# Loading x as bf16 by casting GpSimd DMAs straight into the transpose layout

## The chip, the cores and the metric

The kernel runs on one core of one Trainium2 chip. The time is device microseconds of one execution, as the median of several. The profile's "span", from the first to the last instruction that it records, is about 1.7 us shorter. On names: PE is TensorE, PEld its weight loads, DVE VectorE, ACT ScalarE, POOL GpSimd, SP SyncE.

## The reference

```python
# x: [8, 4096, 192] f32; weight: [8 heads, 7]; w_in: [192, 2048]; w_out: [2048, 192]
w   = softmax(weight, axis=-1)                      # per head, 7 taps
a   = causal_conv(x, w)                             # the 24 channels of a head share 7 taps
h   = a.reshape(32768, 192) @ w_in
out = maximum(0.01 * h, h) @ w_out                  # [32768, 192] f32
```

## The kernel before

The work goes in 32 blocks. A block is 512 positions of two batch rows (`e` = 0, 1). It goes through these steps: load x as f32 (`x_nat`), cast it to bf16 (`x_bf`), transpose it on PE (`ptr`), copy it out of PSUM on DVE (`xt`), convolve on DVE (`yt`), then mm1 on PE (`ph`), leaky ReLU on ACT (`g`), mm2 on PE (`po`), copy on DVE (`o_sb`) and store. x is prepared two blocks ahead of mm1.

```python
def load_x(blk):                       # SP queue, two DMAs of 384 KB, rows of 768 B
    t = stage_pool.tile([128, 2, SUB, D], FP32, name="x_nat")
    for e in range(2):
        nc.sync.dma_start(out=t[:, e, :, :],
            in_=x[2 * rp + e, st * ST : (st + 1) * ST, :].rearrange("(c p) d -> p c d", p=128))
def cast_x(blk, e, copy, half=None):   # x_bf is [128, SUB=4, NCH=3, 2, CH=64]
    copy(out=x_bf[blk][:, s, :, e, :], in_=x_nat[blk][:, e, s, :].rearrange(...))
def transpose_x(blk):                  # 24 transposes; x_bf is the stationary operand
    for s in range(SUB):
        for c in range(NCH):
            for i in range(2):
                ps = slice(i * CH, (i + 1) * CH)
                nc.tensor.transpose(out=ts[i][:, s, c, :],
                    in_=x_bf[blk][ps, s, c, :, :].rearrange("p e k -> p (e k)"),
                    identity=ident[ps, ps])
# ... start: x of blocks 0 and 1, then w_in in four quarters on the SP and ACT queues
load_x(2)                                                   # SP queue, behind w_in
# ... w_in cast on ACT; w_out loaded by a casting GpSimd DMA; 40 warm-up matmuls on PE
for blk in range(NBLK + 1):
    for j in range(STEPS):             # 8 steps
        # ... mm1 and g of blk (two f per step), mm2 of blk - 1
        if blk + 2 < NBLK:
            if j == 0: load_x(blk + 3)
            if 2 <= j < 6: cast_x(blk + 2, j % 2, nc.scalar.copy, half=(j - 2) // 2)
            if j == 7:
                transpose_x(blk + 2)
                evac_x(blk + 2, nc.vector.tensor_copy)
        # ... three of the 21 convolution steps of blk + 1 on DVE
```

Each transpose reads `e` and `k` as one row of 128 elements. This is why `x_bf` keeps them side by side, and why the load must hit this layout if it is to skip the cast.

Of the kernel before, what the change touches and what calls it, by code (L numbers as in the profile page):

```python
# [10 lines left out]
BF16 = mybir.dt.bfloat16  # L11
# [3 lines left out]
def kernel(  # L15
# [8 lines left out]
    nc = tc.nc  # L24
# [10 lines left out]
    CH = 64  # L35
    NCH = D // CH
    ST = 512
    SUB = ST // 128
    NFC = F // 128
    NB = S // ST  # L40
    NBLK = (B // 2) * NB
# [4 lines left out]
    WQ = 4  # L46

    const_pool = ctx.enter_context(tc.tile_pool(name="const", bufs=1))
    stage_pool = ctx.enter_context(tc.tile_pool(name="stage", bufs=3))
    xb_pool = ctx.enter_context(tc.tile_pool(name="xb", bufs=2))  # L50
    xt_pool = ctx.enter_context(tc.tile_pool(name="xt", bufs=2))
    yt_pool = ctx.enter_context(tc.tile_pool(name="yt", bufs=3))
    g_pool = ctx.enter_context(tc.tile_pool(name="g", bufs=3))
# [9 lines left out]
    x_nat, x_bf, xt, ptr = {}, {}, {}, {}  # L63

    def load_x(blk):
        if blk >= NBLK:
            return
        rp, st = divmod(blk, NB)
        t = stage_pool.tile([128, 2, SUB, D], FP32, name="x_nat")
        for e in range(2):  # L70
            nc.sync.dma_start(  # L71
                out=t[:, e, :, :],
                in_=x[2 * rp + e, st * ST : (st + 1) * ST, :].rearrange(
                    "(c p) d -> p c d", p=128
                ),
            )
        x_nat[blk] = t

    def cast_x(blk, e, copy, half=None):
        if blk not in x_bf:  # L80
            x_bf[blk] = xb_pool.tile([128, SUB, NCH, 2, CH], BF16, name="x_bf")
        s = slice(0, SUB) if half is None else slice(half * SUB // 2, (half + 1) * SUB // 2)
        copy(  # L83
            out=x_bf[blk][:, s, :, e, :],
            in_=x_nat[blk][:, e, s, :].rearrange("p s (c k) -> p s c k", c=NCH),
        )

    def transpose_x(blk):


        ts = [psum_o.tile([128, SUB, NCH, CH], BF16, name=f"ptr{i}", tag="po") for i in range(2)]
# [4 lines that stand above are left out]
                    nc.tensor.transpose(  # L96
                        out=ts[i][:, s, c, :],
                        in_=x_bf[blk][ps, s, c, :, :].rearrange("p e k -> p (e k)"),
                        identity=ident[ps, ps],
                    )  # L100
        ptr[blk] = ts

    def evac_x(blk, copy):
        rp, st = divmod(blk, NB)
        if st == 0:
            xt[rp] = xt_pool.tile([128, NCH, HALO + S], BF16, name="xt")
            nc.vector.memset(xt[rp][:, :, 0:HALO], 0.0)
        dst = xt[rp][:, :, HALO + st * ST : HALO + (st + 1) * ST].rearrange(
            "p c (s i k) -> p i s c k", s=SUB, i=2
        )  # L110
        for i, t in enumerate(ptr.pop(blk)):
            copy(out=dst[:, i], in_=t)  # L112


    yt = {}

    def conv_jobs(blk):
        rp, st = divmod(blk, NB)
        y = yt_pool.tile([128, NCH, ST], BF16, name="yt")
        yt[blk] = y  # L120
        jobs = []
        for c in range(NCH):
            for k in range(K):
                src = xt[rp][:, c, BASE + k + st * ST : BASE + k + (st + 1) * ST]
                dst = y[:, c, :]
                if k == 0:
                    jobs.append(
                        lambda s=src, d=dst, c=c: nc.vector.tensor_scalar_mul(  # L128
                            d, s, wk[:, c, 0:1]
                        )  # L130
                    )
                else:
                    jobs.append(
                        lambda s=src, d=dst, c=c, k=k: nc.vector.scalar_tensor_tensor(  # L134
                            out=d, in0=s, scalar=wk[:, c, k : k + 1], in1=d,
                            op0=mybir.AluOpType.mult, op1=mybir.AluOpType.add,
                        )
                    )
        return jobs
# [12 lines left out]
    for sign, off in ((1, 0), (-1, GRP - 1)):  # L152
        nc.gpsimd.affine_select(
            out=sel, in_=sel, compare_op=mybir.AluOpType.is_ge, fill=0.0,
# [11 lines left out]
        out=nmax, in_=w8, axis=mybir.AxisListType.X,  # L166
# [3 lines left out]
        out=w8, in_=w8, func=mybir.ActivationFunctionType.Exp, bias=nmax, scale=1.0,  # L170
    )
    nc.vector.tensor_reduce(
        out=ssum, in_=w8, axis=mybir.AxisListType.X, op=mybir.AluOpType.add,
# [5 lines left out]
    for c in range(NCH):  # L179
        nc.tensor.matmul(  # L180
            out=wps[:, 0, c * K : (c + 1) * K],
# [5 lines left out]
        out=wk, in_=wps[:, 0, 0 : NCH * K].rearrange("p (c k) -> p c k", c=NCH)  # L187
# [4 lines left out]
    cast_x(0, 1, nc.scalar.copy)  # L192
    transpose_x(0)
    evac_x(0, nc.vector.tensor_copy)
    for job in conv_jobs(0):
        job()

    w_stage = g_pool.tile([128, NCH, F], FP32, name="w_stage", tag="g")
    for q in range(WQ):
        for e in range(2):  # L200
            fs = slice(q * F // WQ, (q + 1) * F // WQ)
            (nc.sync, nc.scalar)[e].dma_start(
                out=w_stage[e * CH : (e + 1) * CH, :, fs],
                in_=moe_w_in[:, fs].rearrange("(c p) f -> p c f", p=CH),
            )
    load_x(2)

    cast_x(1, 0, nc.scalar.copy)
    cast_x(1, 1, nc.scalar.copy)
    transpose_x(1)  # L210
    evac_x(1, nc.scalar.copy)

    w_in = const_pool.tile([128, NCH, F], BF16)
# [6 lines left out]
    nc.gpsimd.tensor_copy(out=pjunk, in_=w_stage[0:1, NCH - 1, F - 1 : F])  # L220
    w_out = const_pool.tile([128, NFC, D], BF16)
    nc.gpsimd.dma_start(out=w_out, in_=moe_w_out.rearrange("(c p) d -> p c d", p=128))  # L222


    wa = psum_h.tile([128, 2, ST], FP32, name="warm", tag="ph")
    NWARM = 40
    for i in range(NWARM):
        nc.tensor.matmul(  # L228
            out=wa[:, 0, :], lhsT=ident, rhs=xt[0][:, 0, HALO : HALO + ST],
# [6 lines left out]
    def mm1(blk, f):  # L236
        y = yt[blk]
        ph = psum_h.tile([128, 2, ST], FP32, name="ph", tag="ph")
        for c in range(NCH):
            for e in range(2):  # L240
                ps = slice(e * CH, (e + 1) * CH)
                nc.tensor.matmul(  # L242
                    out=ph[:, e, :],
                    lhsT=w_in[ps, c, f * 128 : (f + 1) * 128],
                    rhs=y[ps, c, :],
                    start=(c == 0),
                    stop=(c == NCH - 1),
                )
        return nc.scalar.activation(  # L249
            out=g[blk][:, f, :, :], in_=ph,  # L250
            func=mybir.ActivationFunctionType.Prelu, alpha=0.01,
        )
# [25 lines left out]
    def mm2(n):  # L278


        if n <= LAST:
            for fc in range(NFC if n < LAST else LAG):
                if n < LAST:
                    mm2_one(0, n, fc)
                t1 = n * NFC + fc - LAG
                if t1 >= 0:
                    mm2_one(1, *divmod(t1, NFC))
                    if t1 % NFC == NFC - 1:
                        evac_o(t1 // NFC)
        if n >= LAST:  # L290
            for fc in range(NFC):
                mm2_one(None, n, fc)
            evac_o(n)
# [16 lines left out]
    for blk in range(NBLK + 1):  # L310
        if blk < NBLK:
            g[blk] = g_pool.tile([128, NFC, 2, ST], BF16, name="g", tag="g")
        jobs = conv_jobs(blk + 1) if blk + 1 < NBLK else []
        for j in range(STEPS):
            n = (blk - 1) * STEPS + j
            if blk < NBLK:
                for f in range(FPS * j, FPS * (j + 1)):
                    act = mm1(blk, f)
                    if f == FPS * j:
                        seal[n] = act.ins.name  # L320
            if n >= 0:
                mm2(n)
            if blk + 2 < NBLK:
                if j == 0:
                    load_x(blk + 3)
                if 2 <= j < 6:
                    cast_x(blk + 2, j % 2, nc.scalar.copy, half=(j - 2) // 2)
                if j == 7:
                    transpose_x(blk + 2)
                    evac_x(blk + 2, nc.vector.tensor_copy)  # L330
            for job in jobs[3 * j : 3 * (j + 1)]:
                job()

# [29 lines left out]
```

## Time and profile before

| | before |
|---|---|
| time, median of 3 | 718.55 us (718.36 to 719.08) |
| span of the profiled run | 717.5 us |
| PE / DVE / ACT / POOL busy | 98 / 79 / 77 / 1% |
| one block in steady state | 21.31 us |

First the page: its busy line, and the engine line of its chain of waits (the work that ended last, followed backwards).

```profile
PE 699.9 (98%) x11933; PEld 606.1 (84%) x11934; DVE 567.0 (79%) x1002; ACT 554.9 (77%) x644; POOL 3.7 (1%) x11
...
PE 94%; DMA 3%; ACT 2%; SPq 0%; issue 0%; DVE 0%; ACTq 0%
```

PE is busy nearly always and is 94% of the chain, so only what shortens PE's own sequence can help. The waits view says who waited for whom: total us, times, longest.

```profile
ACT g L249 <- PE ph L242: 132.6, 247, 1.1
PE ph L242 <- ACT g L249: 3.6, 7, 1.2
```

ACT waits for PE by 132.6 us, and PE for ACT by 3.6 us in the whole run. Spare ACT time is therefore worth nothing in steady state. The chain in order of time (start, length, what) marks one point in each block:

```profile
64.06 1.39 PE po L260 x32
...
639.43 1.36 PE po L260 x32
660.74 1.36 PE po L260 x32
```

From 64.06 to 660.74 are 28 blocks, 596.68 / 28 = 21.310 us each, "the period".

The one stretch where ACT leads is block 0, which has no mm2. The timeline (start, length, engine, line, operation, operands, count) shows its ACT work:

```profile
23.86 1.47 ACT L216 CAST w_in<-w_stage 128x1536 bf16<-128x1536 f32 x1 [1.01 <-DMA w_stage<-in_moe_w_in_dram]
25.24 5.80 ACT L249 ACTIVATE g<-ph 128x1024 bf16<-128x1024 f32 x6
30.94 0.50 ACT L83 CAST x_bf<-x_nat 128x384 bf16<-128x384 f32 x1
31.34 1.94 ACT L249 ACTIVATE g<-ph 128x1024 bf16<-128x1024 f32 x2
33.16 0.52 ACT L83 CAST x_bf<-x_nat 128x384 bf16<-128x384 f32 x1
...
38.00 5.87 ACT L249 ACTIVATE g<-ph 128x1024 bf16<-128x1024 f32 x6
```

The last quarter of w_in is cast at 23.86 us and the activations start at 25.24. Four x casts of block 2 sit between them.

### The profile page before, as it was taken

The numbers are of one execution on the slowest core, as the hardware profiler recorded it, in microseconds if no ns is written. First come the engines' busy times: TensorE is split into PE (matmuls) and PEld (weight loads), VectorE is DVE, ScalarE is ACT, GpSimd is POOL, SyncE is SP. The second block draws the span as 40 slices with busy tenths as digits, with TensorE's granted clock in tenths as the row PEclk, the third lists the DMA queues.
The fourth block names the chain that finished last, engine by engine and source line by source line (L and its number), as shares of the span: only waits on it lengthen the run. The fifth ranks groups of instructions, "written<-read, shape, count | busy, mean of one in ns | idle before, by whom it ended". The sixth has DMA issues, their size and how long they took to land.

```text
span 717.5 us, 26122 instructions
## 1 busy us (share of the span) xinstructions
PE 699.9 (98%) x11933; PEld 606.1 (84%) x11934; DVE 567.0 (79%) x1002; ACT 554.9 (77%) x644; POOL 3.7 (1%) x11
## 2 busy tenths in 40 slices
PE   4899999999999999999999999999999999999998
PEld 2367888888888888888888888888888888888887
DVE  6968888888888888888888888888888888888812
ACT  3887888877788877788887788887778887778771
POOL 1000000000000000000000000000000000000000
PEclk9999999999999999999999999999999999999999
DMA  9902211222221222321222221222222132211112
GB/s 234 206 13 79 79 60 65 86 84 79 90 68 47 90 79 79 90 79 46 80 79 90 79 80 59 67 82 87 79 89 63 52 90 80 79 46 36 45 38 67
DMA packets 72463, 55.95 MB, mean 78 GB/s; under 512 B 5280, under 2 KB 70816, under 8 KB 72352
## 3 DMA queue, kind: packets, MB, share of 16 engines
q1 hardware_dynamic: 69440, 51.92, 23.9%
q10 hardware_dynamic: 848, 1.57, 0.9%
q0 software_dynamic: 2064, 0.79, 0.9%
q8 instruction: 93, 1.52, 0.9%
q14 instruction: 18, 0.15, 0.1%
HBM read 29.88 MB, written 25.17 MB: 77 GB/s over the span
## 4 chain that ended last, share of the span: by engine, by line
PE 94%; DMA 3%; ACT 2%; SPq 0%; issue 0%; DVE 0%; ACTq 0%
PE po L260 47%; PE ph L242 45%; DMA w_stage<-in_moe_w_in_dram 2%; ACT g L249 2%; PE ptr L96 1%; DMA x_nat<-in_x_dram 1%; ACT x_bf L83 0%; ACT w_in L216 0%; SPq L71 0%; DVE o_sb L302 0%; ACTq L216 0%
## 5 line engine op out<-in xcount | busy, mean ns | idle before, releaser
L249 ACT ACTIVATE g<-ph 128x1024 bf16<-128x1024 f32 x512 | 496.3, 1021 | 132.6 <-PE ph L242 132.6
L134 DVE SCALAR_TENSOR_TENSOR yt<-xt,wk,yt 128x512 bf16<-128x512 bf16 x576 | 431.5, 749 | 14.0
L260 PEld LDWEIGHTS <-g 64*128 64x128 bf16 (+1 forms) x8048 | 375.2, 94 | 32.1 <-issue 0.2
L260 PE MATMUL po<-w_out,g 64*128 64x192 bf16 (+1 forms) x8048 | 399.3, 243 | 0.0
L242 PE MATMUL ph<-yt,w_in 64*128 64x512 bf16 x3072 | 392.9, 376 | 4.3 <-ACT g L249 3.6
L242 PEld LDWEIGHTS <-w_in 64*128 64x128 bf16 x3072 | 233.2, 94 | 59.2 <-issue 9.2
L302 DVE COPY o_sb<-po 128x192 f32<-128x192 f32 x256 | 91.6, 358 | 106.5 <-PE po L260 103.8
L83 ACT CAST x_bf<-x_nat 128x384 bf16<-128x384 f32 (+1 forms) x123 | 64.0, 521 | 6.2 <-DMA x_nat<-in_x_dram 6.2
L112 DVE COPY xt<-ptr 128x768 bf16<-128x768 bf16 x62 | 31.7, 553 | 22.2 <-PE ptr L96 22.2
L128 DVE TENSOR_SCALAR yt<-xt,wk 128x512 bf16<-128x512 bf16 x96 | 33.3, 347 | 0.1
L96 PE MATMUL ptr<-ident,x_bf 64*128 64x64 bf16 x768 | 19.2, 193 | 5.5 <-ACT x_bf L83 5.5
L96 PEld LDWEIGHTS <-x_bf 64*128 64x128 bf16 x768 | 17.6, 97 | 5.9 <-ACT x_bf L83 5.7
L228 PE MATMUL warm<-xt,ident 128*128 128x512 bf16 x39 | 10.9, 445 | 0.2 <-issue 0.2
L216 ACT CAST w_in<-w_stage 128x1536 bf16<-128x1536 f32 x4 | 5.9, 1472 | 5.3 <-DMA w_stage<-in_moe_w_in_dram 5.3
L228 PEld LDWEIGHTS <-ident 128*128 128x128 bf16 x40 | 4.4, 113 | 6.3 <-issue 3.0
L180 PE MATMUL wps<-w,sel 8*128 8x7 f32 x6 | 1.4, 354 | 4.1 <-DVE w L177 4.1
L180 PEld LDWEIGHTS wps<-w,sel 8*128 8x128 f32 x6 | 1.4, 321 | 4.1 <-issue 4.1
L160 ACT ACT_TABLE_LOAD x1 | 1.3, 1283 | 1.5 <-PEq L347 1.5
L112 ACT COPY xt<-ptr 128x768 bf16<-128x768 bf16 x2 | 1.5, 802 | 0.9 <-PE ptr L96 0.9
L186 DVE COPY wk<-wps 128x21 f32<-128x21 f32 x1 | 0.2, 182 | 1.6 <-PE wps L180 1.6
L222 POOL DMA_DIRECT2D w_out<-in_moe_w_out_dram x1 | 1.3, 1264 | 0.0
L165 DVE TENSOR_REDUCE nmax<-w 8x1 f32<-8x7 f32 x1 | 0.1, 147 | 1.3 <-DMA w<-in_weight_dram 1.3
(18 smaller groups left out, 4.8 us busy)
## 6 DMA issues: line engine op xcount, KB each, us to landing
x_nat<-in_x_dram SPq DMA_DIRECT2D x64, 384.0 KB, 4.4
out_dram<-o_sb SPq DMA_DIRECT2D x128, 192.0 KB, 2.0
w_stage<-in_moe_w_in_dram SPq DMA_DIRECT2D x4, 384.0 KB, 10.3
w_stage<-in_moe_w_in_dram ACTq DMA_DIRECT2D x4, 384.0 KB, 14.1
w_out<-in_moe_w_out_dram POOLq DMA_DIRECT2D x1, 768.0 KB, 16.0
w<-in_weight_dram ACTq DMA_DIRECT2D x1, 0.2 KB
```

Source lines behind the costliest of these rows:

```text
L83: copy(out=x_bf[blk][:, s, :, e, :], in_=x_nat[blk][:, e, s, :].rearrange("p s (c k) -> p s c k", c=NCH),)
L96: nc.tensor.transpose(out=ts[i][:, s, c, :], in_=x_bf[blk][ps, s, c, :, :].rearrange("p e k -> p (e k)"), identity=ident[ps, ps],)
L112: copy(out=dst[:, i], in_=t)
L128: lambda s=src, d=dst, c=c: nc.vector.tensor_scalar_mul(d, s, wk[:, c, 0:1])
L134: lambda s=src, d=dst, c=c, k=k: nc.vector.scalar_tensor_tensor(out=d, in0=s, scalar=wk[:, c, k : k + 1], in1=d, op0=mybir.AluOpType.mult, ...
L180: nc.tensor.matmul(out=wps[:, 0, c * K : (c + 1) * K], lhsT=sel[:, c, :, :].rearrange("h e k -> h (e k)"), rhs=w8, start=True, stop=True,)
L216: nc.scalar.copy(out=w_in[:, :, fs], in_=w_stage[:, :, fs])
L228: nc.tensor.matmul(out=wa[:, 0, :], lhsT=ident, rhs=xt[0][:, 0, HALO : HALO + ST], start=(i == 0), stop=(i == NWARM - 1),)
L242: nc.tensor.matmul(out=ph[:, e, :], lhsT=w_in[ps, c, f * 128 : (f + 1) * 128], rhs=y[ps, c, :], start=(c == 0), stop=(c == NCH - 1),)
L249: return nc.scalar.activation(out=g[blk][:, f, :, :], in_=ph, func=mybir.ActivationFunctionType.Prelu, alpha=0.01,)
L260: ins = nc.tensor.matmul(out=po[m], lhsT=g[b][ps, fc, e, s * 128 : (s + 1) * 128], rhs=w_out[ps, fc, :], start=(rt != 1 and fc == 0), stop ...
L302: nc.vector.tensor_copy(out=o_sb[:, n % 2, :], in_=po.pop(n))
```

## The change

Its intent is to take 61 us of casts off ACT, one of the three f32 staging buffers off SBUF, and a load off the busy start.

```diff
-    stage_pool = ... name="stage", bufs=3
-    xb_pool = ... name="xb", bufs=2
+    stage_pool = ... name="stage", bufs=2
+    xb_pool = ... name="xb", bufs=3
+    def load_cast_x(blk):
+        ...
+        for s in range(SUB):
+            for e in range(2):
+                t0 = st * ST + s * 128
+                nc.gpsimd.dma_start(
+                    out=x_bf[blk][:, s, :, e, :],
+                    in_=x[2 * rp + e, t0 : t0 + 128, :].rearrange("p (c k) -> p c k", c=NCH),
+                )
-    load_x(2)                                  # after the w_in loads
     nc.gpsimd.dma_start(out=w_out, ...)
+    load_cast_x(2)
+    load_cast_x(3)
             if blk + 2 < NBLK:
-                if j == 0:
-                    load_x(blk + 3)
-                if 2 <= j < 6:
-                    cast_x(blk + 2, j % 2, nc.scalar.copy, half=(j - 2) // 2)
                 if j == 7:
                     transpose_x(blk + 2)
                     evac_x(blk + 2, nc.vector.tensor_copy)
+                    load_cast_x(blk + 4)
```

A block now takes eight GpSimd DMAs, one for each sub-block `s` and batch row `e`. Each moves 384 pieces of 256 B read and 128 B written.

More of the change, by code (lines that the diff above doesn't have):

```diff
@@ L48 @@
     const_pool = ctx.enter_context(tc.tile_pool(name="const", bufs=1))
-    stage_pool = ctx.enter_context(tc.tile_pool(name="stage", bufs=3))
-    xb_pool = ctx.enter_context(tc.tile_pool(name="xb", bufs=2))
+    stage_pool = ctx.enter_context(tc.tile_pool(name="stage", bufs=2))
+    xb_pool = ctx.enter_context(tc.tile_pool(name="xb", bufs=3))
     xt_pool = ctx.enter_context(tc.tile_pool(name="xt", bufs=2))
@@ L112, in evac_x @@
             copy(out=dst[:, i], in_=t)
+    def load_cast_x(blk):
+        if blk >= NBLK:
+            return
+        rp, st = divmod(blk, NB)
+        x_bf[blk] = xb_pool.tile([128, SUB, NCH, 2, CH], BF16, name="x_bf")
+        for s in range(SUB):
[5 more added lines that the diff above has]
+                )
     yt = {}
```

## The prediction

> **What bounds the kernel.** TensorE. The page gives PE 98% busy, and the chain of waits is 94% PE. In the chain one block repeats every 21.3 us (64.06, 85.40, 106.70) with only PE work in it. In the waits view PE waits 3.6 us for `g` in the whole run, ACT 132.6 us for PE: in steady state ACT follows. DVE is busy 17.7 us of each block (windows view), 3.6 us of slack.
>
> The exception is the start. In the timeline from 25.2 to 43.9 us (block 0, without mm2) ACT is always busy: 16 `g` activations of 0.97 us and four x casts of 0.50 to 0.56 us, and PE waits for it. Before that the last quarter of w_in arrives at 23.8 us; its DMA shares the engines with the x load of block 2.
>
> **What the change removes.**
> - 120 ACT casts of 0.51 us, 61 us. 59 of them lie where ACT waits for PE: worth 0. The four in block 0 are on the chain: 2.1 us.
> - The early x load of block 2, so w_in lands sooner: at most 0.7 us, as the warm-up matmuls hold PE until 23.7 us.
> - Together at most 2.5 us: the convolution of block 1 ends on DVE at 38.5 us whatever ACT does, and mm1 of block 1 (now at 41.07) needs it.
>
> **What it adds.**
> - 8 GpSimd DMAs per block. The w_out issue took 1.26 us for 2048 row pieces; I estimate 1 us each, 8 to 10 us per block, on an idle engine.
> - 3072 pieces per block (256 B read, 128 B written) instead of 1024 of 768 B. The w_out pieces took 49 ns each while sharing the engines; so 3072 x 49 / 16 = 9.4 us per block (estimate), beside 2.5 us of stores. DMA share rises from 2 to 5 or 6 tenths; it would limit only at over 95 ns per piece.
> - Latency: with three x_bf buffers a load is issued about two blocks ahead, so none in steady state.
>
> **Where it can hurt.** x of block 2 now queues behind w_out (issued at 18.8 us). I estimate w_out done near 26 us and x of block 2 at 32 to 37 us; its transposes want it at 38 to 40 us. Each us later stalls PE by one, once.
>
> Second, the port that DVE shares with GpSimd. The Trainium skill ("SBUF — State Buffer", section "Who interferes with whom") says DVE copies and tensor-scalar operations in 2-port modes and GpSimd exclude each other, and that software descriptor writes wait for it. This trace shows one software DMA only; the DVE operations beside it kept their 0.78 us. I expect what is lost here to fit in the slack.
>
> **Prediction: 716.8 us**, range 714.5 to 721.5. Faster by over 2%: 0.01; within 2%: 0.93; slower by over 2%: 0.06.
>
> **What would show it.** ACT busy falls by 61 us and its waits for PE grow as much. The block period stays 21.3 us. POOL busy rises to 250 us or more. Block 0's ACT run ends about 2.5 us sooner, and the transposes of block 2 don't wait for a DMA. DMA share 5 to 6 tenths.
>
> **What would make it wrong.** Pieces costing over 95 ns each (a DMA-bound block); GpSimd descriptor work over 21 us per block; DVE slowed by over 3.6 us per block; x of block 2 landing after 45 us. Each shows as PE waiting for x_bf from DMA or yt from DVE.

## The result

| | before | after |
|---|---|---|
| time, median | 718.57 us (4 runs) | 719.45 us (4 runs, 718.91 to 721.36) |
| ratio of means, 95% interval | | 1.0016 (0.9996 to 1.0036) |
| the same again, 11 and 6 runs | 719.36 us | 719.59 us; 1.0008 (0.9992 to 1.0023) |
| span of the profiled run | 717.5 us | 717.1 us |
| period of a block | 21.310 us | 21.386 us |

A ratio is the mean time of one kernel's fast runs over that of the other's in the same rounds, so it is not quite the quotient of the medians. The time did not move: the change is the same as before within 0.4% either way.

The profile after, in the same views. The page's busy line and chain:

```profile
PE 701.7 (98%) x11933; PEld 581.9 (81%) x11934; DVE 569.3 (79%) x1002; ACT 507.5 (71%) x524; POOL 185.4 (26%) x251
...
PE 96%; ACT 2%; DMA 1%; SPq 0%; issue 0%; ACTq 0%; DVE 0%
```

The waits:

```profile
ACT g L264 <- PE ph L257: 180.9, 247, 1.3
PE ph L257 <- ACT g L264: 1.6, 7, 0.5
```

ACT's busy time fell by 554.9 - 507.5 = 47.4 us and its wait for PE grew by 48.3 us. This is the trade of ACT work for ACT idleness that the view of before announced. The chain's marks:

```profile
61.57 1.38 PE po L275 x32
...
638.99 1.36 PE po L275 x32
660.37 1.36 PE po L275 x32
```

This is the most telling view. At the first mark the changed kernel is 64.06 - 61.57 = 2.49 us ahead, and at the last one only 660.74 - 660.37 = 0.37 us. So it did win time at the start (how much of the 2.49 us is chance is taken up under "The start") and then lost 2.1 us in the 28 blocks: 598.80 / 28 = 21.386 us each, 76 ns too many. A result of "the same" hides a gain and a loss of about equal size.

The ACT timeline of block 0 shows the gain:

```profile
23.88 17.43 ACT L264 ACTIVATE g<-ph 128x1024 bf16<-128x1024 f32 x18
```

Eighteen activations run without a break, from 23.88 us on. The loss in the 28 blocks is in one place. Here is the chain over the end of a block, before:

```profile
486.00 1.29 PE ph L242 x12
487.30 1.27 PE po L260 x32
488.57 0.34 PE ptr L96 x21
488.91 0.03 PE ph L242
...
490.26 1.36 PE po L260 x32
```

and after:

```profile
485.02 1.29 PE ph L257 x12
486.31 1.29 PE po L275 x32
487.60 0.46 PE ptr L96 x22
488.07 1.29 PE ph L257 x12
489.36 1.36 PE po L275 x32
```

From the mm2 group ahead of the transposes to the next mm2 group it took 490.26 - 487.30 = 2.96 us before and 489.36 - 486.31 = 3.05 us after. The rest of the block is unchanged: in the marks, 468.95 to 487.30 before against 467.97 to 486.31 after, 18.35 and 18.34 us. So the transposes became slower, although their number and form are the same, and no wait for a DMA is shown. Their view by line gives the one difference, first before, then after (operation, count, duration in ns min/median/max, first and last start):

```profile
L96 PEldq EVENT_SEMAPHORE  x1: 51/51/51, 6.2 to 6.2; - x1
```

```profile
L96 PEldq EVENT_SEMAPHORE  x121: 51/51/51, 6.2 to 658.7; - x121
```

There are 120 more semaphore instructions of 51 ns in PE's weight-load stream, which is 4 for each of 30 blocks. The instruction listing of the built program (from building the kernels, not from a trace) says why. Before, the transposes' weight loads carry no wait for x; PE has already waited for the same ACT counter. After, the first weight load of each sub-block waits for two DMAs, its `e` = 0 and its `e` = 1 load. An instruction with two such waits appears in the trace with a separate semaphore instruction ahead of it. The data had long landed: a load's median time to landing is 2.8 us, and it is issued two blocks ahead.

### The profile page after: what moved, and what is told of

The parts are those of the page before. It is cut to its first block, busy times and chain, and to the rows that moved or that the text cites. A ratio compares the mean times of both kernels' runs of the same rounds, so it can differ in the third digit from the quotient of the medians.

```text
span 717.1 us, 26275 instructions
## 1 busy us (share of the span) xinstructions
PE 701.7 (98%) x11933; PEld 581.9 (81%) x11934; DVE 569.3 (79%) x1002; ACT 507.5 (71%) x524; POOL 185.4 (26%) x251
## 3 DMA queue, kind: packets, MB, share of 16 engines
q0 software_dynamic: 98064, 12.60, 27.2%
## 4 chain that ended last, share of the span: by engine, by line
PE 96%; ACT 2%; DMA 1%; SPq 0%; issue 0%; ACTq 0%; DVE 0%
PE po L275 47%; PE ph L257 45%; ACT g L264 2%; PE ptr L96 2%; PE warm L243 1%; DMA x_nat<-in_x_dram 1%; ACT x_bf L83 0%; SPq L71 0%; ACTq L216 0%; DVE o_sb L317 0%
## 5 line engine op out<-in xcount | busy, mean ns | idle before, releaser
L275 PEld LDWEIGHTS <-g 64*128 64x128 bf16 (+1 forms) x8048 | 369.9, 94 | 37.4 <-issue 0.2
L275 PE MATMUL po<-w_out,g 64*128 64x192 bf16 (+1 forms) x8048 | 394.1, 243 | 0.0
L257 PE MATMUL ph<-yt,w_in 64*128 64x512 bf16 x3072 | 387.7, 376 | 2.4 <-ACT g L264 1.6
L123 POOL DMA_DIRECT2D x_bf<-in_x_dram x240 | 181.8, 763 | 400.0 <-PE ptr L96 381.4
L257 PEld LDWEIGHTS <-w_in 64*128 64x128 bf16 x3072 | 207.1, 94 | 78.2 <-issue 7.1
L142 DVE TENSOR_SCALAR yt<-xt,wk 128x512 bf16<-128x512 bf16 x96 | 35.7, 372 | 0.1
L96 PE MATMUL ptr<-ident,x_bf 64*128 64x64 bf16 x768 | 20.8, 193 | 5.2 <-ACT x_bf L83 5.2
L96 PEld LDWEIGHTS <-x_bf 64*128 64x128 bf16 x768 | 19.2, 96 | 5.8 <-ACT x_bf L83 5.4
L83 ACT CAST x_bf<-x_nat 128x768 bf16<-128x768 f32 x3 | 2.4, 832 | 5.9 <-DMA x_nat<-in_x_dram 5.9
```

The costliest lines, as they stand in the source:

```text
L96: nc.tensor.transpose(out=ts[i][:, s, c, :], in_=x_bf[blk][ps, s, c, :, :].rearrange("p e k -> p (e k)"), identity=ident[ps, ps],)
L123: nc.gpsimd.dma_start(out=x_bf[blk][:, s, :, e, :], in_=x[2 * rp + e, t0 : t0 + 128, :].rearrange("p (c k) -> p c k", c=NCH),)
L142: lambda s=src, d=dst, c=c: nc.vector.tensor_scalar_mul(d, s, wk[:, c, 0:1])
L257: nc.tensor.matmul(out=ph[:, e, :], lhsT=w_in[ps, c, f * 128 : (f + 1) * 128], rhs=y[ps, c, :], start=(c == 0), stop=(c == NCH - 1),)
L275: ins = nc.tensor.matmul(out=po[m], lhsT=g[b][ps, fc, e, s * 128 : (s + 1) * 128], rhs=w_out[ps, fc, :], start=(rt != 1 and fc == 0), stop ...
```

## The experiments

The theory (A) is that the start wins time, and that the double waits at the transposes give it back. The rivals were: B, the many small writes or the descriptor work disturb PE or DVE; C, the number of DMAs or of waits counts, double or not; and chance in the traces. Ten runs followed, two of them repeats without an edit. All gave correct results.

| run | DMAs per block | double waits per block | period, us | excess over 21.310, ns | excess per double wait, ns |
|---|---|---|---|---|---|
| before, two traces | 2, staged | 0 | 21.310, 21.310 | 0 | |
| the change, two traces | 8 | 4, far apart | 21.386, 21.378 | 76, 68 | 18 |
| c12 | 12 | 0 | 21.310 | 0 | |
| c24 | 24 | 0 | 21.310 | 0 | |
| e6 | 6 | 3, close | 21.447 | 137 | 46 |
| h16 | 16 | 8, in close pairs | 21.757 | 447 | 56 |
| d24 | 24 | 12, close | 22.365 | 1055 | 88 |
| traffic | 2, staged, and 8 unread | 0 | 21.310 | 0 | |

### The change again (after_again)

No edit.

> The changed kernel once more, for more rounds and a second trace. Theory A (the start wins 2.5 us, then four extra semaphore instructions per block on the TensorE queue give it back): block period again 21.38 us against 21.31 before, 121 semaphore instructions at the transposes, the mark at which block 1's first g ends again about 42 us. Rival B (chance: the trace of before was a fast one or that of after a slow one): the period moves back towards 21.31. Time within 0.3% of before under both.

Period 21.378, 121 semaphore instructions, first mark at 61.60 us. The loss is not chance.

### One wait per weight load: c12

```diff
-            for e in range(2):
-                    out=x_bf[blk][:, s, :, e, :],
-                    in_=x[2 * rp + e, t0 : t0 + 128, :].rearrange("p (c k) -> p c k", c=NCH),
+            for c in range(NCH):
+                    out=x_bf[blk][:, s, c, :, :],
+                    in_=x[2 * rp : 2 * rp + 2, t0 : t0 + 128, c * CH : (c + 1) * CH]
+                        .rearrange("e p k -> p e k"),
```

Each DMA now brings what one pair of transposes reads, both batch rows of one channel chunk. Pieces, bytes and layout stay.

> Twelve casting DMAs per block instead of eight, each for one sub-block and one channel chunk with both batch rows, so that the first weight load of each transpose pair waits for one DMA only and never for two. Pieces, bytes and layout as in the change. Theory A (each second DMA wait costs a separate semaphore instruction on the TensorE queue, about 19 ns): no such instructions in blocks 2 and later, block period back at 21.31 us, span about 715.0, time about 2.2 us under the changed kernel. Rival B (the many 128 B writes disturb TensorE's reads): period stays 21.38. Rival C (every wait on a DMA costs, also the single one): 12 waits instead of 8, period 21.42 or more. GpSimd 12 x 0.6 to 0.8 us per block, no limit.

```profile
L96 PEldq EVENT_SEMAPHORE  x1: 51/51/51, 6.2 to 6.2; - x1
```

```profile
61.96 1.39 PE po L277 x32
...
658.64 1.36 PE po L277 x32
```

The 120 instructions are gone and the period is (658.64 - 61.96) / 28 = 21.310 us. The time is 717.15 us against 719.36, ratio 0.9971 (0.9959 to 0.9983). It beats both kernels, by 0.3%: clear of noise, but far under 2%. B and C would both have kept the loss.

### Twice the double waits: h16

```diff
+                for i in range(2):
+                    t0 = st * ST + s * 128 + i * CH
-                    out=x_bf[blk][:, s, :, e, :],
-                    in_=x[2 * rp + e, t0 : t0 + 128, :]...
+                    out=x_bf[blk][i * CH : (i + 1) * CH, s, :, e, :],
+                    in_=x[2 * rp + e, t0 : t0 + CH, :]...
```

> Sixteen casting DMAs per block, each for 64 partitions, so that eight weight loads per block wait for two DMAs instead of four. Theory A: about 241 semaphore instructions at the transposes, period 21.46 us (twice the 76 ns of excess), span about 2.1 us over that of the changed kernel. Rival B (disturbance by the writes): same pieces and bytes, period stays 21.38. GpSimd at 16 x 0.77 = 12.3 us per block is no limit under either.

```profile
L96 PEldq EVENT_SEMAPHORE  x241: 51/51/51, 6.2 to 671.9; - x121
```

```profile
64.34 1.38 PE po L276 x32
...
673.53 1.36 PE po L276 x32
```

The count is as expected, the size is not: the period is (673.53 - 64.34) / 28 = 21.757 us, 447 ns of excess instead of 152, and the time 730.42 us, ratio 1.0157 (1.0144 to 1.0171). The double waits stand here at two neighbouring weight loads. The chain shows PE running dry amid the transposes:

```profile
497.34 0.36 PE ptr L96 x12
497.70 0.12 issue
497.82 0.49 PE ptr L96 x11
```

"issue" is time for which the profile shows no wait. My figure of 19 ns for each was therefore not a constant.

### The same number of DMAs, single or double waits: c24 and d24

c24 is c12 with each DMA split into the two halves of 64 partitions, so that every weight load waits for exactly one DMA. d24 splits c12's DMAs by batch row instead, `out=x_bf[blk][:, s, c, e, :]`, so that 12 weight loads wait for two. Both have 24 DMAs per block and the same pieces and bytes.

> Twenty-four casting DMAs per block, each for 64 partitions, one sub-block and one channel chunk with both batch rows: every weight load of the transposes waits for exactly one DMA. It separates the sixteen-DMA run's slowness (period 21.75 us) into its two parts. Theory A (double waits): 24 single waits cost nothing, no extra semaphore instructions, period 21.31, span 715 to 716. Rival C (number of DMAs, or DMAs over half the partitions, or waits at neighbouring weight loads): period 21.75 us or more. GpSimd needs 24 x 0.7 to 0.75 us = 17 to 18 us per block, near its limit of 21.3; if that is over, TensorE waits for DMA.

> Twenty-four casting DMAs per block as in the run with 24 single waits, but each for one sub-block, one channel chunk and one batch row over all 128 partitions, so that twelve weight loads per block wait for two DMAs. Same number of DMAs, same pieces and bytes; only the pairing of DMAs with weight loads differs. Theory A: 361 semaphore instructions, period well over 21.31: 21.54 us if each costs 19 ns as with four per block, up to 22.1 us if those beyond four cost 90 ns each, as the step from four to eight suggests (21.386 to 21.75). Rival C (number of DMAs or of waits): period 21.31, as with 24 single waits.

```profile
L96 PEldq EVENT_SEMAPHORE  x1: 51/51/51, 6.2 to 6.2; - x1
```

```profile
61.57 1.39 PE po L278 x32
...
658.24 1.36 PE po L278 x32
```

```profile
L96 PEldq EVENT_SEMAPHORE  x361: 51/51/51, 6.2 to 688.7; - x181
```

```profile
64.06 1.38 PE po L276 x32
...
690.29 1.36 PE po L276 x32
```

The first two fences are c24: period 21.310 us with 24 single waits, no cost at all, time 717.29 us, ratio 0.9974 (0.9959 to 0.9989). The other two are d24: (690.29 - 64.06) / 28 = 22.365 us, time 748.74 us, ratio 1.0411 (1.0395 to 1.0426). The two move the same pieces in the same number of DMAs. They differ in how the pieces are grouped (c24: 64 partitions, both rows; d24: 128 partitions, one row), and with that in how many DMAs a weight load waits for. The partitions alone don't explain it: h16, with 64, is slow and c24 is not; d24, with 128, is slow and c12 is not. This settles it against C. The excess of d24 is above the 22.1 us that I had given as the upper end.

### Few, but close: e6

```diff
+        for c in range(NCH):
+            for e in range(2):
+                    out=x_bf[blk][:, :, c, e, :],
+                    in_=x[2 * rp + e, st * ST : (st + 1) * ST, c * CH : (c + 1) * CH]
+                        .rearrange("(s p) k -> p s k", p=128),
```

> Six casting DMAs per block, each for one channel chunk and one batch row and all four sub-blocks: three double waits per block, at the first three weight-load pairs of the transposes, two matmul pairs apart. Theory A: 91 semaphore instructions, period 21.31 to 21.37 us, at most that of the changed kernel less one quarter of its excess; the cost may be less if the first ones hide behind queued matmuls. Rival C (single waits or number of DMAs): fewer DMAs than the changed kernel, so 21.31 to 21.38, which alone doesn't tell them apart; it is a point of the dose curve.

```profile
62.21 1.38 PE po L276 x32
...
662.72 1.36 PE po L276 x32
```

The expectation missed. Fewer DMAs and fewer double waits than in the change (91 semaphore instructions), yet the period is 21.447 us, and the time 721.31 us, ratio 1.0030 (1.0013 to 1.0046). The three stand at weight loads four instructions apart, where the change's four are twelve apart. So distance matters as well as number: 46 ns each here against 18 there. Distance alone does not set it either: the twelve of d24 stand four instructions apart too, and cost 88 ns each. I read this as PE's queue of ready work hiding a semaphore instruction when there is time to refill it in between. That reading is only argued; the runs show the costs and the gap in h16, not the queue.

### Traffic without the waits: traffic

```diff
 (kernel before)
+                    load_junk_x(blk + 2)   # load_cast_x into a tile that nobody reads, bufs=1
```

> The kernel before with 240 casting GpSimd DMAs added, the same pieces as in the change, into a buffer that nobody reads. They run on their own pace, about 10 us per block's worth, so in the first 300 us they are denser than in the changed kernel, and the staged loads run beside them. Rival B (the small writes, or GpSimd's descriptor work, slow TensorE or DVE enough to matter): period above 21.31 us in the first 300 us, back to 21.31 afterwards. Theory A: 21.31 throughout, no semaphore instructions at the transposes, span within 0.5 us of 717.5. VectorE's tensor-scalar operations should take longer while the DMAs are issued.

```profile
63.19 1.39 PE po L275 x32
...
659.87 1.36 PE po L275 x32
```

```profile
100.00:200.00 100.00, 100.00 (x1782) 88.66 (x1779) 83.15 (x148) 79.80 (x93) 63.67 (x85) 1.00 0.92 119
500.00:600.00 100.00, 100.00 (x1781) 88.68 (x1779) 82.50 (x147) 80.14 (x94) 0.00 (x0) 1.00 0.25 77
```

The second fence is the table by stretch: the busy us of each engine, granted clock, DMA share, GB/s. From 100 to 200 us the added DMAs keep POOL busy for 63.67 us and the DMA share at 0.92; from 500 us on they are over. The period is 21.310 us throughout, and the time is that of before, ratio 0.9997 (0.9981 to 1.0013). B falls. One sign of it was in the trace of the change already: its last x load is issued near 602 us, and the block from 638.99 to 660.37 still takes 21.38 us.

A cost to DVE does show, off the chain. These are the tensor-scalar operations in the trace before, and in that of the change:

```profile
L128 DVE TENSOR_SCALAR yt<-xt,wk x96: 343/347/352, 8.5 to 673.7; 128x512 bf16<-128x512 bf16 x96
```

```profile
L142 DVE TENSOR_SCALAR yt<-xt,wk x96: 343/349/608, 8.3 to 673.3; 128x512 bf16<-128x512 bf16 x96
```

The longest grew from 352 to 608 ns, and in the traffic run to 668. There the mean was 392 ns from 30 to 300 us, while the DMAs were issued, and 347 ns from 305 us on, when they were over. In c24 the mean is 407 ns instead of 347, over 96 operations 5.8 us in the whole run. The `scalar_tensor_tensor` operations did not change (741 to 754 ns in the change, 741 to 753 before). This agrees with the Trainium skill, "SBUF — State Buffer", section "Who interferes with whom", by which a tensor-scalar operation in a 2-port mode is kept out while GpSimd has the port, and an operation with two SBUF inputs only meets GpSimd's reads. That the tensor-scalar operations run in such a mode is not shown by a run. DVE had 3.6 us of slack per block, so it cost nothing.

### The start: before_b, b2cast, b_hold

b2cast is the kernel before with the casting DMAs for block 2 alone. b_hold keeps all its casts. Both make the SP queue wait for w_in before the staged loads:

```diff
-    load_x(2)
+    hj = const_pool.tile([1, 1], FP32, name="hj")
+    nc.sync.dma_start(out=hj, in_=w_stage[127:128, NCH - 1, F - 1 : F])   # waits for w_in
+    load_x(2)                                                            # b_hold only
```

> The kernel before, for a second trace of it. It tells how much of the difference at the start is the same in every run. Period 21.31 us is expected again. The first g of block 0 began at 25.24 us in the first trace of it, at 23.88 and 23.92 in the two of the changed kernel; theory A (part of the start's win is w_in landing sooner): 25.0 to 25.5 again. Rival (that part is chance in when x of block 1 lands): anywhere from 23.9 to 26.

> The kernel before, with block 2 alone loaded by casting DMAs and the staged loads of blocks 3 and later held back until w_in has landed. Theory A: the start wins its full 2.5 us (no ACT casts in block 0: 1.2 us, w_in earlier: 1.3 us), the period stays at 21.31 us, span about 715.0. If the staged loads, now later, come too late for block 3's casts, ACT waits for DMA near 44 us, without cost to TensorE. Rival B (the start's win is an accident of this trace): span 717.5.

> The kernel before with one edit: the x loads of block 2 and later wait on the SP queue until w_in has landed. The casts on ACT stay. Theory A: w_in lands about 1.3 us sooner, as in the changed kernel, so the first g begins near 24 us, the four casts in block 0 still cost about 1.2 us, the period stays at 21.31: span 716.0 to 716.5. If the casts of block 0 then wait for x (landing after 31 us) ACT shows that wait and part of the win is lost.

| run | first g, us | first mark, us | between |
|---|---|---|---|
| before, before_b, traffic | 25.24, 24.80, 24.37 | 64.06, 63.62, 63.19 | 38.82, 38.82, 38.82 |
| b_hold | 24.28 | 63.11 | 38.83 |
| change, again, c12, c24 | 23.88, 23.92, 24.35, 23.95 | 61.57, 61.60, 61.96, 61.57 | 37.69, 37.68, 37.61, 37.62 |
| e6, h16, d24 | 24.46, 26.27, 25.14 | 62.21, 64.34, 64.06 | 37.75, 38.07, 38.92 |
| b2cast | 24.72 | none at this block | |

before_b, the kernel before unedited, took 718.63 us, ratio 0.9994 (0.9979 to 1.0009), with the period of 21.310 us again. The last column repeats to 0.01 us in the first two rows and in each pair of the third (the fourth has its own double waits in it): without the four casts the stage is 38.82 - 37.61 = 1.21 us shorter (0.07 less in the change, which has a double-wait transpose group in it). So a cast in block 0 costs 0.30 us of the chain and not its 0.51: it overlaps both its neighbours by 0.10 us.

The first column varies from run to run, also with what the change doesn't touch: in h16, the latest, the transposes of block 1 start at 13.63 us, in the change at 11.53. before_b, at 24.80, missed the expected 25.0 to 25.5 and fell in the rival's range. The mean of the three traces of kernels that load x of block 2 early is 24.80 us. That of all eight that load it by casting DMAs is 24.59, with a spread of 2.4, so these traces do not show what w_in gains. The times suggest a gain: c12 and c24 took 2.1 and 1.9 us less than before, by their ratios, and the casts are 1.2 of it. That leaves an estimated 0.7 to 0.9 us, whose cause is not shown.

b2cast took 717.31 us, ratio 0.9974 (0.9962 to 0.9987): its period is 21.309 us (marks 84.06 to 659.40, 27 blocks), and it keeps a win at the start without the loss. In its trace g starts only 0.52 us sooner than in before and the span is 716.0 us, not the expected 715.0; four of its six runs have 715.2. That separates the two halves of the theory.

b_hold is inconclusive. w_in landed sooner (its last cast starts at 21.88 us instead of 23.86, 23.42 or 22.99), but the first activation then waited for PE:

```profile
12.64 10.35 PE L230 MATMUL warm<-xt,ident 128*128 128x512 bf16 x38 [0.22 <-issue]
24.28 5.81 ACT L251 ACTIVATE g<-ph 128x1024 bf16<-128x1024 f32 x6 [0.92 <-PE ph L244]
```

The warm-up matmuls end at 12.64 + 10.35 = 22.99 us and hold mm1, which then waits 0.32 us more for the convolution of block 0 on DVE (1.24 us in c12). So with w_in sooner, these two come next. The time was 718.11 us, ratio 0.9986 (0.9969 to 1.0002), which fits a small gain as well as none.

## Why the prediction was right

"Within 2%" and the time, 719.45 us in a range of 714.5 to 721.5, came out, and with it the main reason: PE bounds the kernel, and in steady state ACT's casts are off the chain. That the time stayed in the range is partly luck: the loss that was not foreseen happened to be small with this cut of the DMAs. The same bytes cut as in h16 or d24 took 730.42 and 748.74 us, both outside it. Point by point:

- **ACT.** Predicted: busy time down 61 us, waits up as much. Measured: 47.4 and 48.3 us. The direction held and the size was off; it fits that the casts overlap their neighbours and that busy time counts an overlap once.
- **Start.** Predicted: ACT's run in block 0 ends about 2.5 us sooner. It ended at 43.87 us (38.00 + 5.87) and now at 41.31 (23.88 + 17.43), 2.56 sooner. Part of that is chance between traces. Of its terms the casts were mis-sized, 1.2 instead of 2.1 us; the one for w_in, at most 0.7 us, is not settled by the traces, and an estimated 0.7 to 0.9 is left for all but the casts.
- **x of block 2 in time.** Predicted to land at 32 to 37 us. The eight DMAs are issued by 27.9 us and no x load took over 7.1 us to land, so by 35.0 us; the transposes start at 38.13 and wait for no DMA.
- **DMA cost.** Predicted 49 ns a piece, a share of 5 or 6 tenths. Measured: 27.2% of 16 engines over 717.1 us for 98064 packets (w_out among them), 31.8 ns each on average, and a share of about 4 tenths.
- **GpSimd.** Predicted 1 us for each DMA, 250 us or more. Measured 763 ns and 185.4 us.
- **Block period.** Predicted: it stays at 21.3 us. This is the step that failed. It became 21.386 us. Of 2.1 us lost in 28 blocks the prediction has no term, as it looked for PE waiting for data and not for the cost of the wait instructions themselves. This is why the point estimate of 716.8 us, which counted only the gain, was 2.65 us under the median; the loss is 2.1 of it.

What stays open: some executions of the changed kernel take 2.2 to 3.1 us outside the span, where all executions of the kernel before take 1.7 to 1.8; two of c24's four do so as well, and none of c12's. No run tells why. It accounts for 0.3 to 0.6 us of the mean. Nor is it shown what in PE makes close double waits dearer than distant ones, or what the start gained beyond the casts.

## What to carry to other kernels

When a kernel is bound by one engine, count the instructions that a change puts into that engine's own stream, semaphore waits included; a wait whose data is long there can still cost. Cut DMAs along the lines of the consumer's instructions, so that each instruction waits for one of them: here 24 such DMAs per block cost nothing, while 6 that met in pairs cost 137 ns. And when a change moves nothing, compare the traces at several marks along the run: the difference grew from 0 to 2.5 us and shrank to 0.4.

## What the Trainium skill lacked or had wrong

- No page gives what the extra semaphore instruction ahead of a weight load with two DMA waits (51 ns in the trace) costs a busy PE: 18 ns each where 4 stand twelve instructions apart, 46, 56 and 88 ns in the three closer patterns, and 0 for up to 24 single waits. It would belong to "Perfetto Trace Analysis", section "Identifying Dependency Chains", which says that such instructions may stand ahead of one that waits on several engines, without a cost.
- "DMA: Bandwidth & Descriptors", section "Specifications", says that under 512 B a transfer leaves line rate and is a read-modify-write. The first part agrees: 128 B in 31.8 ns against 768 B in 39.5 (23.9% of 16 engines over 717.5 us for 69440 packets of before's x and stores). Whether a read-modify-write is part of the 31.8 ns can't be told from these runs. The page gives no cost per casting piece.
- "SBUF — State Buffer", section "Who interferes with whom", warns of the shared port, and the times fit; it lacks the size for descriptor work: the mean tensor-scalar operation went from 347 to 372 ns with 8 DMAs per block and to 407 with 24. Its opposite warning, that DVE starves the descriptor writes, did not show in the change, whose x issues took 741 to 778 ns. In c24 they took 592 to 1337 ns, and no run tells why.
- No page gives what a cast between two activations adds to a full ACT: a cast of 0.51 us added 0.30 us, as each neighbour overlapped it by 0.10. It would belong to "Perfetto Trace Analysis", section "Optimizing Scalar/DVE Operations", which says that part of an instruction's profiled latency overlaps with the next.
